# Memory attention and a Sinkhorn mixture of experts: the norm's epsilon in a preset column, one reduction for two, and four small products on GpSimd

## The chip, the cores and the metric

The kernel runs on one core of one Trainium2 chip. A core has five engines that work from queues of their own: TensorE (PE in the profile; its weight loads are PEld), VectorE (DVE), ScalarE (ACT), GpSimd (POOL) and SyncE (SP), which here issues the DMAs. Each engine takes its instructions in order; semaphores hold an instruction back until what it needs is done. The metric is device time in microseconds (us) of one execution, less is better.

## The reference

The first half is an attention with a memory, for B = 4 batches, H = 8 heads, S = 576 rows and D = 64 columns. The second half takes its output as the 2304 x 512 input of a mixture of 8 experts, whose router is normalised by Sinkhorn steps. The change lies in the first half, in the norm `mem_norm` and in the two lines that use it.

```python
scores = scale * np.matmul(q, k.transpose(0, 1, 3, 2))      # causal mask, then
a = np.exp(scores - scores.max(-1, keepdims=True))
a /= a.sum(-1, keepdims=True) + 1e-09
local = np.matmul(a, v)
q_p = np.where(q > 0, q, np.exp(q) - 1.0) + 1.0             # phi(q)
mem_ret = np.einsum('bhsd,bhde->bhse', q_p, M_prev)
mem_norm = np.einsum('bhsd,bhd->bhs', q_p, z_prev)[..., None] + 1e-06
g = 1.0 / (1.0 + np.exp(-beta))[None, :, None, None]
out = g * mem_ret / mem_norm + (1 - g) * local
```

## The kernel before

**Tiling.** Attention works on 16 pairs of heads (p = 0 to 15). A pair's 576 rows are four tiles of 128 rows with both heads side by side (128 columns), and a fifth tile in which the 64 left rows of the first head lie on partitions 0 to 63 and those of the second on 64 to 127, each in its own half of the columns, with zeros in the other half. So a per-row number of a pair is a 128 x 9 tile: eight columns for four tiles times two heads, and one for the fifth tile.

**One pair.** `qkt` transposes q and k and splits them into a high and a low part (L231). `phi_` makes phi(q): exp on ACT into `tmp` (L256), min with 1 on DVE (L257), max and add on DVE into `phi` (L258), and then POOL multiplies phi by z into `tmp` again (L261 for four tiles, L265 for the fifth). `nrm` sums `tmp` over the 64 columns (L274, and L277 for the fifth tile), adds 1e-6 (L278), takes the reciprocal (L279) and multiplies by the gate (L280); the result is `rm`. `pv_in` multiplies v by one minus the gate on POOL (L286, `vs`). `scores` multiplies q and k (L303), adds the mask and takes the smallest negated score on DVE (L317, two instructions for each tile of rows), and exponentiates on ACT (L324); `scores_tail` does the same for the fifth tile (L335, L341, L347). ACT writes the sums into `sum`, and the last of them is L347's.

`r_stats` adds 1e-9 to `sum` (L415), multiplies by `rm` (L416, `rms`), takes the reciprocal of the sum (L417, `rv`), and POOL then scales phi by `rms`: the fifth tile into `qn4` (L420, two instructions), the four others in place (L425). `r_trans` transposes `rv` (L433), `qn4` (L434) and the scaled phi (L455) on TensorE; the copies out of PSUM are L436, L452 and L456. The row of `rv` goes through DRAM by DMA and comes back as `rsb` (L447), broadcast over the partitions. `t_a` and `t_b` transpose the exponentials (L361, L379), copied out by L362, L367 and others. `pv` multiplies them with `vs` and the scaled phi with the memory matrix (L470, L475), and `comb`, all on POOL, multiplies by `rsb` (L494), rounds (L497) and subtracts (L498) to get the two parts of the second half's input.

**Order.** Each step carries a phase number, and the list of all steps is sorted by pair plus phase: load -1.6, qkt -0.40, phi_ -0.38, pv_in -0.36, nrm -0.10, scores 0, t_a 0.50, r_stats 0.70, t_b 0.80, r_trans 0.90, pv 0.95 and 1.15, comb 1.45. `w_task`, at 0.5, 1.0, 1.5 and 2.0, splits the first expert's weights on POOL (L115, L116), and from pair 5 on matmuls of the second half (L621, L636) and the router's logits fill in between. This list is the order on TensorE. On the other engines the scheduler chooses an order when the program is built, and it is then fixed.

**Buffers.** `phi`, `rm`, `vs`, `rr` have two buffers each, by the parity of the pair; `tmp` has one.

Of the kernel before, what the change touches and what calls it, by code (L numbers as in the profile page):

```python
# [8 lines left out]
F32 = mybir.dt.float32  # L9
F32R = mybir.dt.float32r  # L10
AF = mybir.ActivationFunctionType
ALU = mybir.AluOpType
AX = mybir.AxisListType
# [4 lines left out]
def kernel(  # L18
# [13 lines left out]
    nc = tc.nc  # L32
# [55 lines left out]
    gcol = ca.tile([128, HP, 9], F32, name="gcol")  # L88
# [82 lines left out]
    def attention():  # L171
        with ExitStack() as actx:
            ap1 = actx.enter_context(tc.tile_pool(name="ap1", bufs=1))
# [4 lines left out]
            qraw, kraw, vraw = (  # L178
                [ap1.tile([128, 5, 128], F32, name=f"{x}raw{j}") for j in range(2)] for x in "qkv"
            )  # L180
# [6 lines left out]
            e4t = ap1.tile([128, 2, 64], F32, name="e4t")  # L187
            e4 = ap1.tile([128, 576], F32, name="e4")
            qn4 = ap1.tile([128, 128], F32, name="qn4")

            for t_ in (*qraw, *kraw, *vraw):
                nc.vector.memset(t_[:, 4, :], 0.0)
            for t_ in (*mraw, *zb2, qn4, e4t):
                nc.vector.memset(t_, 0.0)

            st = [dict() for _ in range(NPAIR)]
            half = [slice(0, 64), slice(64, 128)]
# [51 lines left out]
                split_ps(kk[0][:, 576:704], kk[1][:, 576:704], tv[:, 1])  # L249

            def phi_(p):
                tmp = ap1.tile([128, 5, 128], F32, tag="tmp", name="tmp", bufs=1)
                phi = ap1.tile([128, 5, 128], F32, tag="phi", name="phi", bufs=2)
                st[p]["phi"], st[p]["tmp"] = phi, tmp
                zb = zb2[p % 2]
                nc.scalar.activation(out=tmp, in_=qraw[p % 2], func=AF.Exp)  # L256
                nc.vector.tensor_scalar_min(tmp, tmp, 1.0)  # L257
                nc.vector.scalar_tensor_tensor(  # L258
                    out=phi, in0=qraw[p % 2], scalar=0.0, in1=tmp, op0=ALU.max, op1=ALU.add
                )  # L260
                nc.gpsimd.tensor_tensor(  # L261
                    out=tmp[:, 0:4], in0=phi[:, 0:4],
                    in1=zb[:, 0:1].to_broadcast([128, 4, 128]), op=ALU.mult,
                )
                nc.gpsimd.tensor_tensor(  # L265
                    out=tmp[:, 4], in0=phi[:, 4], in1=zb[:, 1], op=ALU.mult
                )

            def nrm(p):
                hp = p % HP  # L270
                tmp = st[p].pop("tmp")
                rm = ap1.tile([128, 9], F32, tag="rm", name="rm", bufs=2)
                st[p]["rm"] = rm
                nc.vector.reduce_sum(  # L274
                    rm[:, 0:8], tmp[:, 0:4].rearrange("p t (h d) -> p (t h) d", h=2), axis=AX.X
                )
                nc.vector.reduce_sum(rm[:, 8:9], tmp[:, 4], axis=AX.X)  # L277
                nc.vector.tensor_scalar_add(rm, rm, 1e-6)  # L278
                nc.vector.reciprocal(out=rm, in_=rm)  # L279
                nc.vector.tensor_tensor(out=rm, in0=rm, in1=gcol[:, hp], op=ALU.mult)  # L280

            def pv_in(p):
                hp = p % HP
# [127 lines left out]
            def r_stats(p):  # L411
                phi = st[p]["phi"]
                rr = ap1.tile([128, 3, 9], F32, tag="rr", name="rr", bufs=2)
                den, rms, rv = (rr[:, j] for j in range(3))
                nc.vector.tensor_scalar_add(den, st[p]["sum"], 1e-9)  # L415
                nc.vector.tensor_tensor(out=rms, in0=st[p]["rm"], in1=den, op=ALU.mult)  # L416
                nc.vector.reciprocal(out=rv, in_=den)  # L417
                st[p]["rr"] = rr
                for h in range(2):
                    nc.gpsimd.tensor_tensor(  # L420
                        out=qn4[half[h], half[h]], in0=phi[half[h], 4, half[h]],
                        in1=rms[half[h], 8:9].to_broadcast([64, 64]), op=ALU.mult,
                    )
                ph = phi[:, 0:4].rearrange("p t (h d) -> p (t h) d", h=2)
                nc.gpsimd.tensor_tensor(  # L425
                    out=ph, in0=ph, in1=rms[:, 0:8].unsqueeze(2).to_broadcast([128, 8, 64]),
                    op=ALU.mult,
                )
# [60 lines left out]
            def comb(p, grp):  # L489
# [11 lines left out]

            atoms = [
                (-1.6, load), (-0.40, qkt), (-0.38, phi_), (-0.36, pv_in), (-0.10, nrm),
                (0.00, lambda p: scores(p, (3,))), (0.01, lambda p: scores(p, (2,))),
                (0.30, lambda p: scores(p, (1, 0))), (0.31, scores_tail),
                (0.50, t_a), (0.80, t_b), (0.70, r_stats), (0.90, r_trans),
                (0.95, lambda p: pv(p, 0)), (1.15, lambda p: pv(p, 1)),
                (1.45, lambda p: comb(p, 0)), (1.46, lambda p: comb(p, 1)),
# [437 lines left out]

    setup()
    attention()
    front.close()
    experts()  # L950
# [30 lines left out]
```

## Time and profile before

| what | value |
|---|---|
| device time, median of 3 runs | 1772.59 us (1772.06 to 1774.39) |
| span of the profiled execution, first to last instruction | 1770.6 us |
| device time of the runs less the span | 2.0 us |
| mean granted TensorE clock, as a share of full speed | 0.996 |
| TensorE busy | 1723.7 us, 97% of the span |
| DVE busy | 1289.0 us, 73% |
| POOL busy | 1166.0 us, 66% |
| ACT busy | 685.7 us, 39% |
| attention, by the trace | 0 to about 272 us |

The trace has the profiled execution's own time as its span; the runs lie 2.0 us above it, which is what lies around the first and the last instruction. A busy share here is an average over a first half in which five engines hand work to each other and a second half that is nearly all matmuls, so it says nothing of a single stage.

### The profile page before, as it was taken

Reading aid. Unit: us, or ns where it says so; the run is one execution under the profiler, and the core shown is the slowest. Engines: PE = TensorE matmul, PEld = TensorE weight load, DVE = VectorE, ACT = ScalarE, POOL = GpSimd, SP = SyncE. Lnnn points to the kernel's source line nnn. Section 1 sums busy time; section 2 is a strip of 40 time slices with the busy share of each in tenths; the row PEclk is TensorE's granted clock in tenths of the full one; section 3 lists DMA queues with packets and bytes.
Section 4 is the critical chain, followed back from the end, with each engine's and each line's share of the span. In section 5 each row is a group of like instructions: output and inputs, shape, how many; then the busy total and the mean of one; then the engine's idle time right before and its main releaser. Section 6 shows DMA issues by size and latency. Waiting matters only on the chain.

```text
span 1770.6 us, 26969 instructions
## 1 busy us (share of the span) xinstructions
PE 1723.7 (97%) x9381; PEld 1522.5 (86%) x9381; DVE 1289.0 (73%) x2371; ACT 685.7 (39%) x1550; POOL 1166.0 (66%) x1113
## 2 busy tenths in 40 slices
PE   5899999999999999999999999999999999999999
PEld 4677777889999999888899999998898999999998
DVE  6887873787777777767777777777667777777776
ACT  4766762233333333333333333333333333333332
POOL 4655543567777777676677777776676777777773
PEclk8999999999999999999999999999999999999999
DMA  4443414222222222214222222222142222222221
GB/s 109 105 103 96 114 41 149 57 70 71 72 66 61 65 72 72 72 49 142 72 71 61 65 66 72 72 72 72 48 143 72 65 61 66 72 72 72 72 60 48
DMA packets 154888, 135.55 MB, mean 77 GB/s; under 512 B 71424, under 2 KB 121728, under 8 KB 154752
## 3 DMA queue, kind: packets, MB, share of 16 engines
q1 hardware_dynamic: 154320, 133.05, 25.0%
q8 instruction: 74, 1.21, 0.3%
q10 hardware_dynamic: 432, 0.79, 0.1%
q14 instruction: 62, 0.51, 0.1%
HBM read 124.28 MB, written 9.51 MB: 76 GB/s over the span
## 4 chain that ended last, share of the span: by engine, by line
PE 81%; POOL 5%; DVE 4%; issue 4%; DMA 2%; ACT 2%; SPq 1%; POOLq 0%; ACTq 0%; DVEq 0%
PE s L636 40%; PE s L805 27%; PE f L805 9%; PE x L470 1%; ACT e L324 1%; DMA rsb<-rd 1%; PE s L303 1%; DVE hhl L790 1%; POOL tl L710 1%; POOL phi L425 1%; POOL w1l L756 1%; DVE acc L877 0%; PE s L621 0%; PE f L636 0%; POOL w2l L779 0%
## 5 line engine op out<-in xcount | busy, mean ns | idle before, releaser
L756 POOL TENSOR_TENSOR w1l<-raw,w1h 128x512 fp32r<-128x512 f32 x263 | 368.2, 1414 | 395.1 <-ACT w1h L755 394.9
L878 DVE SCALAR_TENSOR_TENSOR acc<-s,P,acc 128x512 f32<-128x512 f32 x504 | 369.2, 745 | 133.5 <-PE s L636 131.1
L636 PE MATMUL s<-w2h,hhh 128*128 128x512 f32 x1116 | 435.5, 390 | 6.0 <-DVE acc L878 5.9
L636 PE MATMUL s<-w2h,hhl 128*128 128x512 f32 x1116 | 436.1, 391 | 0.0
L636 PE MATMUL s<-w2l,hhh 128*128 128x512 f32 x1116 | 435.8, 391 | 0.0
L836 DVE TENSOR_TENSOR temps<-s,temps 128x384 f32<-128x384 f32 x447 | 242.5, 555 | 169.8 <-ACT w1h L755 83.0
L790 DVE SCALAR_TENSOR_TENSOR hhl<-temps,hhh 128x384 fp32r<-128x384 f32 x340 | 306.5, 901 | 0.0
L779 POOL TENSOR_TENSOR w2l<-raw,w2h 128x512 fp32r<-128x512 f32 x186 | 292.7, 1595 | 11.9 <-ACT w2h L778 11.9
L789 ACT ACTIVATE hhh<-temps 128x384 fp32r<-128x384 f32 x340 | 178.7, 526 | 297.8 <-DVE temps L836 289.9
L636 PEld LDWEIGHTS s<-w2h,hhh 128*128 128x128 f32 x1116 | 209.6, 188 | 50.6 <-DVE acc L878 9.5
L636 PEld LDWEIGHTS s<-w2h,hhl 128*128 128x128 f32 x1116 | 209.4, 188 | 44.0
L636 PEld LDWEIGHTS s<-w2l,hhh 128*128 128x128 f32 x1116 | 209.4, 188 | 41.5
L839 ACT COPY temps<-s 128x384 f32<-128x384 f32 x64 | 30.7, 480 | 413.7 <-PE s L805 412.6
L805 PE MATMUL s<-th,w1l 128*128 128x384 f32 x510 | 170.8, 335 | 1.5 <-POOL w1l L756 1.5
L805 PE MATMUL s<-tl,w1h 128*128 128x384 f32 x510 | 170.7, 335 | 0.8 <-POOL tl L710 0.8
L805 PE MATMUL s<-th,w1h 128*128 128x384 f32 x510 | 170.6, 334 | 0.0
L805 PE MATMUL s<-xh,w1l 128*128 128x384 f32 x480 | 161.7, 337 | 0.5 <-POOL w1l L751 0.5
L805 PE MATMUL s<-xh,w1h 128*128 128x384 f32 x480 | 161.7, 337 | 0.0
L805 PE MATMUL s<-xl,w1h 128*128 128x384 f32 x480 | 161.2, 336 | 0.0
L755 ACT CAST w1h<-raw 128x512 fp32r<-128x512 f32 x263 | 153.7, 615 | 3.7 <-issue 3.0
L836 DVE TENSOR_TENSOR temps<-f,temps 128x384 f32<-128x384 f32 x148 | 80.3, 555 | 55.3 <-PE f L805 26.2
L778 ACT CAST w2h<-raw 128x512 fp32r<-128x512 f32 x186 | 112.1, 607 | 0.0
(220 smaller groups left out, 2895.0 us busy)
## 6 DMA issues: line engine op xcount, KB each, us to landing
raw<-in_moe_w_dram SPq DMA_DIRECT2D x372, 256.0 KB
rsb<-rd SPq DMA_DIRECT2D x32, 144.0 KB
ydr<-wst SPq DMA_DIRECT2D x18, 256.0 KB
acc<-ydr SPq DMA_DIRECT2D x18, 256.0 KB
qraw<-in_q_dram SPq DMA_DIRECT2D x32, 128.0 KB
kraw<-in_k_dram SPq DMA_DIRECT2D x32, 128.0 KB
vraw<-in_v_dram SPq DMA_DIRECT2D x32, 128.0 KB
out_dram<-acc SPq DMA_DIRECT2D x15, 256.0 KB
```

What stands on the lines that cost most here:

```text
L303: nc.tensor.matmul(out=sp[h][:, at:at + w], lhsT=qq[x][half[h], 128 * i:128 * i + 128], rhs=kk[y][half[h], 0:w], start=(a == 0), stop=(a = ...
L636: nc.tensor.matmul(out=pt, lhsT=h_[:, f, cols], rhs=w[:, f], start=(n == 0), stop=(n == 5))
L755: nc.scalar.copy(out=wh[:, i:i + 2], in_=src)
L756: tt(out=wl[:, i:i + 2], in0=src, in1=f32(wh[:, i:i + 2]), op=ALU.subtract)
L778: nc.scalar.copy(out=wh[:, j], in_=raws[j])
L779: nc.gpsimd.tensor_tensor(out=wl[:, j], in0=raws[j], in1=f32(wh[:, j]), op=ALU.subtract)
L789: nc.scalar.activation(out=hh[:, f, c], in_=src, func=AF.Relu)
L790: late.append(lambda: nc.vector.scalar_tensor_tensor(out=hl[:, f, c], in0=src, scalar=0.0, in1=f32(hh[:, f, c]), op0=ALU.max, op1=ALU.subt ...
L805: nc.tensor.matmul(out=pt[:, 0:HT], lhsT=w[:, wi, k], rhs=x[:, k], start=(n == 0), stop=(n == total - 1),)
L836: nc.vector.tensor_tensor(out=o, in0=x, in1=y, op=ALU.add)
L839: nc.scalar.copy(out=X, in_=prod(q, [(0, b11)]))
L878: nc.vector.scalar_tensor_tensor(out=acc[:, j], in0=pt, scalar=P[:, t_, e:e + 1], in1=acc[:, j], op0=ALU.mult, op1=ALU.add,)
```

## The change

`tmp` becomes one tile for the whole attention, 65 columns for each tile and head in place of 64. The 65th column is preset once: 1e-6, and zero for the second half of the fifth tile. `phi_` writes exp straight into `phi` and works there in place, so that `tmp` only holds phi times z; POOL's product for four tiles becomes two instructions (one for each head), since the rows are now 65 apart. `nrm` takes one reduction over all ten groups of 65, which brings the epsilon with it, and adds the two columns of the fifth tile on POOL (128 x 1). Its product with the gate, and in `r_stats` the sum plus 1e-9 and the product with `rm`, go from DVE to POOL. Both reciprocals stay on DVE.

```diff
+            tmp = ap1.tile([128, 5, 2, 65], F32, name="tmp")
...
+            nc.vector.memset(tmp[:, :, :, 64:65], 1e-6)
+            nc.vector.memset(tmp[:, 4, 1, 64:65], 0.0)
...
-                tmp = ap1.tile([128, 5, 128], F32, tag="tmp", name="tmp", bufs=1)
...
-                nc.scalar.activation(out=tmp, in_=qraw[p % 2], func=AF.Exp)
-                nc.vector.tensor_scalar_min(tmp, tmp, 1.0)
+                nc.scalar.activation(out=phi, in_=qraw[p % 2], func=AF.Exp)
+                nc.vector.tensor_scalar_min(phi, phi, 1.0)
                 nc.vector.scalar_tensor_tensor(
-                    out=phi, in0=qraw[p % 2], scalar=0.0, in1=tmp, op0=ALU.max, op1=ALU.add
-                )
+                    out=phi, in0=qraw[p % 2], scalar=0.0, in1=phi, op0=ALU.max, op1=ALU.add
+                )
+                pv_ = phi.rearrange("p t (h d) -> p t h d", h=2)
+                zv = zb.rearrange("p t (h d) -> p t h d", h=2)
+                for h in range(2):
+                    nc.gpsimd.tensor_tensor(
+                        out=tmp[:, 0:4, h, 0:64], in0=pv_[:, 0:4, h],
+                        in1=zv[:, 0:1, h].to_broadcast([128, 4, 64]), op=ALU.mult,
+                    )
                 nc.gpsimd.tensor_tensor(
-                    out=tmp[:, 0:4], in0=phi[:, 0:4],
-                    in1=zb[:, 0:1].to_broadcast([128, 4, 128]), op=ALU.mult,
-                )
-                nc.gpsimd.tensor_tensor(
-                    out=tmp[:, 4], in0=phi[:, 4], in1=zb[:, 1], op=ALU.mult
+                    out=tmp[:, 4, :, 0:64], in0=pv_[:, 4], in1=zv[:, 1], op=ALU.mult
                 )
...
-                rm = ap1.tile([128, 9], F32, tag="rm", name="rm", bufs=2)
+                rm = ap1.tile([128, 10], F32, tag="rm", name="rm", bufs=2)
...
-                nc.vector.reduce_sum(
-                    rm[:, 0:8], tmp[:, 0:4].rearrange("p t (h d) -> p (t h) d", h=2), axis=AX.X
-                )
-                nc.vector.reduce_sum(rm[:, 8:9], tmp[:, 4], axis=AX.X)
-                nc.vector.tensor_scalar_add(rm, rm, 1e-6)
-                nc.vector.reciprocal(out=rm, in_=rm)
-                nc.vector.tensor_tensor(out=rm, in0=rm, in1=gcol[:, hp], op=ALU.mult)
+                nc.vector.reduce_sum(rm, tmp.rearrange("p t h d -> p (t h) d"), axis=AX.X)
+                nc.gpsimd.tensor_tensor(
+                    out=rm[:, 8:9], in0=rm[:, 8:9], in1=rm[:, 9:10], op=ALU.add
+                )
+                nc.vector.reciprocal(out=rm[:, 0:9], in_=rm[:, 0:9])
+                nc.gpsimd.tensor_tensor(
+                    out=rm[:, 0:9], in0=rm[:, 0:9], in1=gcol[:, hp], op=ALU.mult
+                )
...
-                nc.vector.tensor_scalar_add(den, st[p]["sum"], 1e-9)
-                nc.vector.tensor_tensor(out=rms, in0=st[p]["rm"], in1=den, op=ALU.mult)
+                nc.gpsimd.tensor_scalar_add(den, st[p]["sum"], 1e-9)
+                nc.gpsimd.tensor_tensor(out=rms, in0=st[p]["rm"][:, 0:9], in1=den, op=ALU.mult)
                 nc.vector.reciprocal(out=rv, in_=den)
```

The changed program is five lines longer ahead of the attention's steps, so that L256 to L258 of before are L258 to L260 there, L279 is L282, L286 is L291, L317 is L322, L415 to L425 are L420 to L430 and L494 is L499; phi times z is L266 and L270, the one reduction L278, the sum of the two columns L279, the gate on POOL L283. TensorE's order stays as it was. What the scheduler makes of the rest is shown at three places.

POOL's queue at the first two pairs; vs_123 and vs_124 are the products of pairs 0 and 1 (L286), zb_126 belongs to pair 1. Before:

```order
L261 TENSOR_TENSOR tmp<-phi,zb_126 128x512
L265 TENSOR_TENSOR tmp<-phi,zb_126 128x128
L286 TENSOR_TENSOR vs<-vraw_123,ogb 128x640
L286 TENSOR_TENSOR vs<-vraw_124,ogb 128x640
L420 TENSOR_TENSOR qn_136<-phi,rr 64x64 x2
L425 TENSOR_TENSOR phi<-phi,rr 128x512
```

And now:

```order
L279 TENSOR_TENSOR rm<-rm 128x1
L420 TENSOR_SCALAR rr<-sum 128x9
L283 TENSOR_TENSOR rm<-rm,gcol 128x9
L421 TENSOR_TENSOR rr<-rm,rr 128x9
L425 TENSOR_TENSOR qn_136<-phi,rr 64x64 x2
L430 TENSOR_TENSOR phi<-phi,rr 128x512
L291 TENSOR_TENSOR vs<-vraw_123,ogb 128x640
L291 TENSOR_TENSOR vs<-vraw_124,ogb 128x640
L266 TENSOR_TENSOR tmp<-phi,zb_126 128x4x64 x2
L270 TENSOR_TENSOR tmp<-phi,zb_126 128x2x64
```

The scaling of pair 0's phi stands ahead of both products with v, and pair 1's phi times z behind them.

POOL's queue around the scaling of pair 1's phi, from the product with v for pair 2 on; L115 and L116 are the weights, L494 to L498 are `comb` of pair 0. Before:

```order
L286 TENSOR_TENSOR vs<-vraw_123,ogb 128x640
L115 CAST w1h_72<-wst 128x512
L116 TENSOR_TENSOR w1l_73<-wst,w1h_72 128x512
L494 TENSOR_TENSOR xc<-xc,rsb 128x256
L494 TENSOR_TENSOR xc<-xc,rsb 128x320
L497 CAST xh<-xc 128x256
L497 CAST xh<-xc 128x320
L498 TENSOR_TENSOR xl<-xc,xh 128x256
L498 TENSOR_TENSOR xl<-xc,xh 128x320
L420 TENSOR_TENSOR qn_136<-phi,rr 64x64 x2
L425 TENSOR_TENSOR phi<-phi,rr 128x512
```

And now:

```order
L291 TENSOR_TENSOR vs<-vraw_123,ogb 128x640
L115 CAST w1h_72<-wst 128x512
L279 TENSOR_TENSOR rm<-rm 128x1
L116 TENSOR_TENSOR w1l_73<-wst,w1h_72 128x512
L283 TENSOR_TENSOR rm<-rm,gcol 128x9
L115 CAST w1h_72<-wst 128x512
L116 TENSOR_TENSOR w1l_73<-wst,w1h_72 128x512
L420 TENSOR_SCALAR rr<-sum 128x9
L421 TENSOR_TENSOR rr<-rm,rr 128x9
L425 TENSOR_TENSOR qn_136<-phi,rr 64x64 x2
L499 TENSOR_TENSOR xc<-xc,rsb 128x256
L499 TENSOR_TENSOR xc<-xc,rsb 128x320
```

Behind these stand the four other instructions of `comb` of pair 0 (L502, L503), and only then L430, the scaling of pair 1's phi: `comb` went from ahead of pair 1's `qn4` to between it and the rest of phi. L279 of pair 2's norm stands behind a product with v and a cast of weights.

DVE's queue behind the last reduction of scores of pair 5 (L341 and its accumulator); L627 and L632 are the second half's hidden layer, L367 and L362 copies that free PSUM. Before:

```order
L341 ISA mn 128x1
L415 TENSOR_SCALAR rr<-sum 128x9
L416 TENSOR_TENSOR rr<-rm,rr 128x9
L417 RECIPROCAL rr<-rr 128x9
L627 SCALAR_TENSOR_TENSOR hl_77<-f,hh_76 128x512
L367 COPY e_133<-s 128x128
L362 COPY eB<-s 128x3x128 x2
```

And now:

```order
L346 ISA mn 128x1
L422 RECIPROCAL rr<-rr 128x9
L632 SCALAR_TENSOR_TENSOR hl_77<-f,hh_76 128x512
L372 COPY e_133<-s 128x128
L367 COPY eB<-s 128x3x128 x2
```

The reciprocal stands where it stood, but what it reads (`rr`, from L420) now comes from POOL, where L420 stands behind `comb` of the pair ahead.

## Rows read from the trace of the kernel before

**Rows 1.** Busy time of each engine by stretch (us, count), granted clock, DMA.

```profile
20.00:100.00 80.00, 65.15 (x547) 47.50 (x546) 69.16 (x220) 51.85 (x160) 51.73 (x66) 0.94 0.44 107
100.00:272.00 172.00, 167.19 (x1347) 130.05 (x1347) 134.53 (x458) 115.77 (x344) 90.02 (x126) 1.00 0.33 87
272.00:1770.00 1498.00, 1481.83 (x7445) 1337.03 (x7441) 1074.01 (x1650) 510.25 (x1028) 1020.29 (x908) 1.00 0.23 73
```

The columns behind the stretch's length are PE, PEld, DVE, ACT and POOL, then the granted TensorE clock, the DMA share and GB/s.

**Rows 2.** What TensorE waited for, 20 to 100 us: total, times, longest.

```profile
PE s L434 <- POOL qn L420: 6.0, 2, 5.7
PE s L455 <- POOL phi L425: 3.0, 4, 0.8
```

**Rows 3.** Tiles rm and rr on DVE: shortest/median/longest ns of one.

```profile
L416 DVE TENSOR_TENSOR rr<-rm,rr x16: 153/328/1442, 26.6 to 265.0; 128x9 f32<-128x9 f32 x16
...
L278 DVE TENSOR_SCALAR rm<-rm x15: 176/798/1471, 31.1 to 244.5; 128x9 f32<-128x9 f32 x15
```

**Rows 4.** Prices: groups up to 480 us (busy us, mean ns), and one memset.

```profile
L256 ACT ACTIVATE tmp<-qraw 128x640 f32<-128x640 f32 x16 | 11.8, 736 | 14.2 <-DMA kraw<-in_k_dram 7.9 <-DVE rm L277 4.0 <-DMA qraw<-in_q_dram 2.3
L420 POOL TENSOR_TENSOR qn<-phi,rr 64x64 f32<-64x64 f32 x32 | 9.3, 291 | 6.4 <-DVE rr L416 3.4 <-DVE rr L417 1.4
L257 DVE TENSOR_SCALAR tmp<-tmp 128x640 f32<-128x640 f32 x16 | 8.1, 504 | 3.8 <-ACT tmp L256 3.8
...
0.24 0.10 POOL L965 MEMSET const-float32-0.0<- 128x1 f32 x1 [0.24 <-issue]
```

**Rows 5.** Timeline, pair 0: start, us, instruction, [idle before it <- releaser].

```profile
11.94 0.69 DVE L274 TENSOR_REDUCE rm<-tmp 128x8 f32<-128x512 f32 x1 [5.27 <-POOL tmp L261]
...
15.13 0.69 DVE L317 CUSTOM_DVE_ANT_0 e<-s,mask 128x512 f32<-128x512 f32 x1 [0.43 <-PE s L303]
...
26.52 3.02 POOL L286 TENSOR_TENSOR vs<-vraw,ogb 128x640 f32<-128x640 f32 x2 [2.77 <-DVE rm L280]
...
31.34 1.12 PE L455 MATMUL s<-ident,phi 128*128 128x128 f32 x4 [0.65 <-POOL phi L425]
```

**Rows 6.** Timeline, pair 1.

```profile
36.34 0.69 DVE L317 CUSTOM_DVE_ANT_0 e<-s,mask 128x512 f32<-128x512 f32 x1 [0.91 <-PE s L303]
...
40.63 0.41 DVE L317 CUSTOM_DVE_ANT_0 e<-s,mask 128x256 f32<-128x256 f32 x1
...
42.57 1.55 POOL L494 TENSOR_TENSOR xc<-xc,rsb 128x256 f32<-128x256 f32 x2
...
43.95 0.19 ACT L347 ACTIVATION_READ_ACCUMULATOR e<-e,mn 128x1 f32 x1
...
44.82 1.55 POOL L498 TENSOR_TENSOR xl<-xc,xh 128x256 fp32r<-128x256 f32 x2
...
48.31 0.66 PE L455 MATMUL s<-ident,phi 128*128 128x128 f32 x4 [0.79 <-POOL phi L425]
```

**Rows 7.** Timeline, from pair 1's transposes to pair 2's.

```profile
49.00 0.59 ACT L456 COPY qp<-s 128x512 f32<-128x512 f32 x1 [0.91 <-PE s L455]
...
50.60 1.30 POOL L261 TENSOR_TENSOR tmp<-phi,zb 128x512 f32<-128x512 f32 x1 [2.35 <-DVE phi L258]
...
62.14 1.05 POOL L425 TENSOR_TENSOR phi<-phi,rr 128x512 f32<-128x512 f32 x1
```

**Rows 8.** Timeline, pairs 9 and 6.

```profile
167.65 1.55 POOL L498 TENSOR_TENSOR xl<-xc,xh 128x256 fp32r<-128x256 f32 x2
168.34 0.20 DVE L417 RECIPROCAL rr<-rr 128x9 f32<-128x9 f32 x1
...
169.34 0.33 PE L245 MATMUL s<-ident,kraw 128*128 128x128 f32 x1 [0.67 <-DVE e L367]
...
122.24 0.33 PE L245 MATMUL s<-ident,kraw 128*128 128x128 f32 x1 [0.80 <-ACT eB L362]
```

**Rows 9.** Busy time by stretch, columns as in rows 1, in the second half.

```profile
784.00:787.00 3.00, 0.96 (x4) 0.70 (x5) 2.77 (x4) 0.83 (x1) 3.00 (x3) 1.00 0.04 16
787.00:790.00 3.00, 3.00 (x11) 3.00 (x10) 1.16 (x3) 1.30 (x3) 3.00 (x3) 0.51 0.37 118
```

More of the change, by code (lines that the diff above doesn't have):

```diff
@@ L251, in phi_ @@
             def phi_(p):
-                tmp = ap1.tile([128, 5, 128], F32, tag="tmp", name="tmp", bufs=1)
                 phi = ap1.tile([128, 5, 128], F32, tag="phi", name="phi", bufs=2)
-                st[p]["phi"], st[p]["tmp"] = phi, tmp
+                st[p]["phi"] = phi
                 zb = zb2[p % 2]
-                nc.scalar.activation(out=tmp, in_=qraw[p % 2], func=AF.Exp)
-                nc.vector.tensor_scalar_min(tmp, tmp, 1.0)
+                nc.scalar.activation(out=phi, in_=qraw[p % 2], func=AF.Exp)
+                nc.vector.tensor_scalar_min(phi, phi, 1.0)
                 nc.vector.scalar_tensor_tensor(
-                    out=phi, in0=qraw[p % 2], scalar=0.0, in1=tmp, op0=ALU.max, op1=ALU.add
+                    out=phi, in0=qraw[p % 2], scalar=0.0, in1=phi, op0=ALU.max, op1=ALU.add
                 )
-                nc.gpsimd.tensor_tensor(
-                    out=tmp[:, 0:4], in0=phi[:, 0:4],
-                    in1=zb[:, 0:1].to_broadcast([128, 4, 128]), op=ALU.mult,
-                )
-                nc.gpsimd.tensor_tensor(
-                    out=tmp[:, 4], in0=phi[:, 4], in1=zb[:, 1], op=ALU.mult
+                pv_ = phi.rearrange("p t (h d) -> p t h d", h=2)
[5 more added lines that the diff above has]
+                    )
+                nc.gpsimd.tensor_tensor(
+                    out=tmp[:, 4, :, 0:64], in0=pv_[:, 4], in1=zv[:, 1], op=ALU.mult
                 )
@@ L270, in nrm @@
                 hp = p % HP
-                tmp = st[p].pop("tmp")
-                rm = ap1.tile([128, 9], F32, tag="rm", name="rm", bufs=2)
+                rm = ap1.tile([128, 10], F32, tag="rm", name="rm", bufs=2)
                 st[p]["rm"] = rm
-                nc.vector.reduce_sum(
-                    rm[:, 0:8], tmp[:, 0:4].rearrange("p t (h d) -> p (t h) d", h=2), axis=AX.X
-                )
-                nc.vector.reduce_sum(rm[:, 8:9], tmp[:, 4], axis=AX.X)
-                nc.vector.tensor_scalar_add(rm, rm, 1e-6)
-                nc.vector.reciprocal(out=rm, in_=rm)
-                nc.vector.tensor_tensor(out=rm, in0=rm, in1=gcol[:, hp], op=ALU.mult)
+                nc.vector.reduce_sum(rm, tmp.rearrange("p t h d -> p (t h) d"), axis=AX.X)
+                nc.gpsimd.tensor_tensor(
+                    out=rm[:, 8:9], in0=rm[:, 8:9], in1=rm[:, 9:10], op=ALU.add
+                )
+                nc.vector.reciprocal(out=rm[:, 0:9], in_=rm[:, 0:9])
+                nc.gpsimd.tensor_tensor(
+                    out=rm[:, 0:9], in0=rm[:, 0:9], in1=gcol[:, hp], op=ALU.mult
+                )
             def pv_in(p):
```

## The prediction

> **What bounds the kernel now.** I read the busy time by stretch first, to find where a change to attention can still move the end. From 272 us on TensorE is busy 1481.8 of 1498 us [rows 1]; nothing is edited there, so the time moves by what attention's end moves. From 100 to 272 us TensorE is busy 167.2 of 172 us, so 4.8 us at most can be won there. From 20 to 100 us it is idle 14.9 us: there other engines set the pace. Next I read TensorE's waits in that stretch: 9.0 of the 14.9 us are waits for POOL's two scalings of phi, L420 and L425, one of them of 5.7 us [rows 2]. So the chain that decides runs through POOL: phi times z, the products with v, the weights and `comb`, all in one queue with the scalings. The reader is to see that DVE's small products are not what TensorE waits for by name; they are a step of the way to L420.
>
> **What is taken away.** Two of DVE's small instructions are odd: L416 takes 153 ns at best but 328 at the median and 1442 at most, L278 176, 798 and 1471 [rows 3]. Their shapes never change: L416 of pair 0, one of the long ones, began at 26.6, just behind the start of POOL's L286 at 26.52 [rows 3, 5]. I read them as held until the running POOL instruction ends, and the change takes L278, L280, L415 and L416 off DVE, 64 instructions over the 16 pairs. L277 goes into the longer reduction. What a stall cost TensorE is at most the stretch by which the next step was late, and that is counted below, place by place.
>
> **What is added on POOL.** Four small products for each pair. No row shows a POOL product of nine columns. Below it is bounded by the memset of 128x1, 0.10 us, above by L420's 64x64 at 0.29 [rows 4]. I take 0.15 and 0.07 for the hand-over, 0.22 in all, since nine columns are nearer to one than to 64. Phi times z becomes two instructions of 256 columns for one of 512 at 1.30 [rows 7]; two of 256 and 320 take 1.55 (L494 [rows 6]), so I take 1.5: +0.2.
>
> **Pair 0.** POOL's scaling waited at 26.52 for DVE's L280, then did both products with v (3.02 us), and only then L420 and L425; L455 began at 31.34 [rows 5]. Now the scaling is ahead of both: -3.0. L274 stood on DVE ahead of the splits of q and k and held them 5.27 us [rows 5]; it now stands behind them. Pair 0's first scores, at 15.13, come about 1.1 earlier, and the gates that POOL waits for with them. L455 of pair 0 at 27.2: -4.1.
>
> **Pair 1.** The two products with v (3.0) now run after L430, to 30.2, and pair 1's phi times z (2.0) after them, to 32.2. The one reduction (0.7, as L274) waits for that and stands on DVE ahead of the score reductions, which so begin at 33.7, not 36.34 [rows 6]. Four of them end at 35.9, pair 2's phi at 36.7, its product with z at 38.7. Then POOL does vs of pair 2 (1.5, half of L286's two) and a cast of weights (0.6, from the 0.7 that `comb`'s two casts of 576 columns fill between L494 and L498 [rows 6]) ahead of L279, whose result DVE's reciprocal waits for; behind the reciprocal stand the last score reductions: 41.3, where they began at 40.63 [rows 6]. So the lead is gone: +0.7. The last sum, at 44.14 (43.95 and 0.19), comes at about 44.9. L420, L421 and L425 take 0.22, 0.22 and 0.66: 46.0. Now `comb` of pair 0 is behind them and takes 3.8 to 3.9 (before it ran from 42.57 to 46.37, while the sums were made and divided: that was its cover [rows 6]). 49.9, and L430 takes 1.05 to 51.0: L455 of pair 1 at 51.1 for 48.31 [rows 6]: **+2.8**. Bounds: 0 if the DMA-fed parts come earlier and comb starts at once, 3.9 if all of comb is late.
>
> **Pair 2.** From 48.3 to 63.2 (62.14 and 1.05) POOL is busy but for 2.35 us ahead of phi times z [rows 7]. That gap is a chain: L455, then L258, which writes the `phi` that L455 has read. L256 and L257 had been done into `tmp` meanwhile. Now they write `phi` too, so they come behind L455 and L456: 0.59, then 0.74 and 0.50 [rows 4, 7], less what L257 overlapped: +1.1. The product with z adds 0.2, the four small ones 0.9, the hand-over to vs 0.4: **+2.6**, and **+0.5** for pair 3 by the same chain with a little slack; none for pair 4, whose queue has no weights.
>
> **Pairs 5 to 15.** L422 stands where L417 stood, but waits for L420, which stands behind `comb`. At pair 9 L498 ends at 169.20 (167.65 and 1.55), while L417 began at 168.34 and L245 waited at 169.34 for L367 behind it [rows 8]. With L420's 0.22 and a hand-over L422 begins at 169.5: 1.15 later, and what stands behind it (L632, L372, L367) too, for which L245 waits. Pairs 5, 8 and 12 have the same order and L417 ahead of comb's end by like amounts: 4 x 1.15 = 4.6 (bounds 0, if the copies have slack, and 6). Two pairs with 0.1 of slack in the scaling lose 0.3 each. Given back: pairs 6 and 10, where L245 waited 0.80 at 122.24 [rows 8] for copies that DVE's stalled products held, 0.8 each, and 0.6 at the last pair. **+3.0** net.
>
> **The clock.** After 3 us in which TensorE was busy only 0.96, the next 3 us were granted 0.51 of full speed, 1.2 GHz, with TensorE busy throughout: 1.5 us lost [rows 9]. Now there is a gap of nearly 4 us ahead of pair 1's L455, which had 0.79. I take one more such stretch, a little longer: **+1.7** (0 to 4).
>
> **Sum.** 2.8 + 2.6 + 0.5 + 3.0 + 1.7 = 10.6 on the profiled span of 1770.6: 1781.2, and 2.0 around it: **1783.2** against the median of 1772.59. The second half begins later by as much and is otherwise the same.
>
> **A rule weighed.** The nearest rows gave 0.15 us for a small product on POOL, about what DVE needs unstalled (0.153 to 0.176 [rows 3]). The Trainium skill, "GPSIMD Engine Reference", section Key points, has VectorE about twice as fast at elementwise work. By that a product would be an estimated 0.35, and where some 15 of them lie on the path the sum would be 3 us more, 1786. No row here has the same product on both engines.
>
> **The rivals.**
>
> *Faster, about 1764.* The stalls of DVE go (a long L416 or L278 costs up to 1.3 over its shortest [rows 3]), and pair 0's lead of 4.1 stays, because DVE's queue, free of them, keeps POOL fed. Then -4.1, three stalls of 1.1 among pairs 1 to 3, -1.6 at pairs 6 and 10: -9.0. It decides if POOL has over 1 us of slack a pair in 30 to 63 us. For it: the stalls are real, and 9 us of waits there have POOL's name [rows 2]. Against it: in pair 2's loop POOL's only slack is a wait on `phi` [rows 7], which the change makes longer. The Trainium skill, "SBUF — State Buffer", section Who interferes with whom, bears on this rival: a DVE product with two SBUF inputs, or a copy-like one in a two-port mode, and a GpSimd instruction lock each other out, a reduction does not. The trace agrees as far as L416 and L278 stretch to eight and nine times their shortest [rows 3].
>
> *No change, about 1773.* The pace from 60 us on is TensorE's own, and what POOL loses in pairs 1 and 2 is filled from its list, or pair 0's lead of 4.1 pays for pair 2. For it: 97% busy from 100 us on [rows 1]. Against it: TensorE's order is fixed, and L455 is in it ahead of pair 2's products.
>
> *Much slower, about 1789.* TensorE's gaps ahead of L455 lower the clock in three or four pairs, at 1.5 to 2 each [rows 9], and comb's 3.9 is late in pair 2 as well.
>
> **How the numbers follow.** The forecast's own terms, with their bounds, go from 1776 to 1789. I give it 0.56, much slower 0.08, no change 0.2, faster 0.16. To leave out no more than 2 in 10 the range must reach through no change and a little into the faster case: 1768 to 1788. What a measurement can tell is about 0.2%, 3.5 us: faster than 1769.0 has 0.15, within it 0.2, slower than 1776.1 has 0.65.
>
> **What would show it.** After: TensorE idle before pair 0's L460 at about 27 rather than 31; the scaling of pair 1 (L425, L430) split by `comb`, with L460 of pair 1 near 51 after a wait of some 4 us for POOL; L258 of pair 3 behind L460 of pair 1, and POOL's wait before L266 near 3.4; L422 in pairs 5, 8, 9 and 12 waiting for POOL's L420 and TensorE's transposes of k (L248) waiting for L372; TensorE at half clock once more between 50 and 60. Small POOL products of 0.10 to 0.29. I am wrong if L460 of pair 2 comes no later than 63.2, if TensorE is idle under 15 us from 20 to 100, or if the second half begins before 272.

## The result, and the profile after

| | before | changed |
|---|---|---|
| device time, median of 4 runs | 1773.49 us (1772.06 to 1775.50) | 1784.67 us (1783.32 to 1787.42) |
| span of the profiled execution | 1770.6 us | 1782.2 us |

The ratio is 1.0062, with a 95% interval of 1.0048 to 1.0077: slower by 11 us, where 1783.2 had been forecast. From the page of the changed kernel, the span and the row with busy time, share of the span and instructions of each engine:

```profile
span 1782.2 us, 26967 instructions
...
PE 1730.5 (97%) x9381; PEld 1529.0 (86%) x9381; DVE 1259.3 (71%) x2293; ACT 686.2 (39%) x1550; POOL 1180.0 (66%) x1193
```

DVE has 29.7 us less to do and POOL 14.0 more. The shares hardly move, so the page alone would not tell which way the time went. The busy time by stretch does (columns as in rows 1; below the first three rows, the stretches around four gaps):

```profile
20.00:100.00 80.00, 60.72 (x466) 44.26 (x464) 48.85 (x172) 45.05 (x138) 53.57 (x88) 0.89 0.41 97
100.00:272.00 172.00, 164.80 (x1335) 128.42 (x1335) 120.17 (x403) 116.12 (x339) 96.62 (x171) 0.99 0.34 88
272.00:1770.00 1498.00, 1484.26 (x7492) 1339.18 (x7491) 1073.32 (x1666) 515.61 (x1046) 1025.26 (x919) 1.00 0.24 73
23.00:26.00 3.00, 0.00 (x0) 0.00 (x0) 2.86 (x14) 0.46 (x2) 1.80 (x4) 1.00 0.48 111
27.00:33.00 6.00, 5.48 (x26) 3.65 (x28) 1.11 (x2) 1.59 (x3) 5.06 (x7) 0.50 0.25 57
46.00:50.00 4.00, 0.21 (x2) 0.00 (x0) 1.90 (x8) 0.80 (x3) 4.00 (x7) 1.00 0.43 101
51.00:54.00 3.00, 3.00 (x17) 1.77 (x18) 1.32 (x2) 1.59 (x3) 0.27 (x1) 0.50 0.44 107
65.00:67.00 2.00, 0.03 (x1) 0.00 (x0) 0.86 (x3) 1.16 (x5) 1.92 (x4) 1.00 0.06 13
68.00:74.00 6.00, 5.14 (x23) 3.19 (x25) 2.07 (x6) 1.59 (x3) 2.03 (x4) 0.50 0.28 66
178.00:179.50 1.50, 0.00 (x0) 0.00 (x0) 0.80 (x3) 0.00 (x0) 1.20 (x5) 1.00 0.62 142
180.25:183.75 3.50, 3.50 (x10) 2.67 (x9) 2.05 (x5) 1.59 (x5) 0.54 (x1) 0.55 0.31 71
```

From 20 to 100 us TensorE is idle 19.3 us (80 less 60.72) against 14.9 in [rows 1], from 100 to 272 us 7.2 against 4.8, and four times a gap is followed by a stretch at half the clock (0.50, 1.2 GHz; the last is 0.55 on average over the window shown). The kernel before had one such stretch in attention, at 26 to 36 us, which answers to the first of the four. What TensorE waited for from 20 to 100 us (total, times, longest; the rows that answer to [rows 2]):

```profile
PE s L460 <- POOL phi L430: 5.6, 3, 4.1
PE s L439 <- POOL qn L425: 4.0, 2, 3.6
PE s L366 <- ACT e L329: 2.8, 2, 2.5
PE s L438 <- DVE rr L422: 2.5, 1, 2.5
```

The places are those of the prediction, in the timeline of the changed kernel at pairs 0, 1 and 2:

```profile
23.95 0.37 POOL L283 TENSOR_TENSOR rm<-rm,gcol 128x9 f32<-128x9 f32 x1 [4.14 <-DVE gcol L152]
...
27.14 0.47 PE L460 MATMUL s<-ident,phi 128*128 128x128 f32 x1 [0.79 <-POOL phi L430]
...
45.51 0.73 POOL L499 TENSOR_TENSOR xc<-xc,rsb 128x256 f32<-128x256 f32 x1
...
49.26 1.04 POOL L430 TENSOR_TENSOR phi<-phi,rr 128x512 f32<-128x512 f32 x1
...
50.36 0.33 PE L460 MATMUL s<-ident,phi 128*128 128x128 f32 x1 [4.14 <-POOL phi L430]
...
53.73 0.74 POOL L266 TENSOR_TENSOR tmp<-phi,zb 128x256 f32<-128x256 f32 x1 [3.43 <-DVE phi L260]
...
57.52 1.55 POOL L291 TENSOR_TENSOR vs<-vraw,ogb 128x640 f32<-128x640 f32 x1 [1.94 <-PE x L475]
...
67.55 0.27 PE L438 MATMUL s<-ident,rr 128*9 128x128 f32 x1 [2.52 <-DVE rr L422]
```

Pair 0 is 4.2 us early (27.14 for 31.34), pair 1 late by 2.05 (50.36 for 48.31 [rows 5, 6]). The transposes of the scaled phi (L455, now L460) mark the way of each pair; their starts in the changed kernel less those of before, each from the one profiled execution (the times of 27 executions of the kernel before lie between 1769.4 and 1776.8 us, so differences of one or two microseconds in the text below are not certain by themselves):

| pair | 0 | 1 | 2 | 3 | 4 | 8 | 9 | 12 | 15 |
|---|---|---|---|---|---|---|---|---|---|
| us | -4.20 | 2.05 | 6.10 | 8.36 | 7.93 | 9.09 | 11.92 | 12.78 | 12.11 |

So 8.4 us are lost up to pair 3, 2.8 at pair 9 alone, and nothing behind attention: 11.6 at the end of the span.

### The profile page after: what moved, and what is told of

It is laid out like the page before. It is cut to its first block, busy times and chain, and to the rows that moved or that the text cites. A ratio compares the mean times of both kernels' runs of the same rounds, so it can differ in the third digit from the quotient of the medians.

```text
span 1782.2 us, 26967 instructions
## 1 busy us (share of the span) xinstructions
PE 1730.5 (97%) x9381; PEld 1529.0 (86%) x9381; DVE 1259.3 (71%) x2293; ACT 686.2 (39%) x1550; POOL 1180.0 (66%) x1193
## 3 DMA queue, kind: packets, MB, share of 16 engines
q8 instruction: 74, 1.21, 0.3%
## 4 chain that ended last, share of the span: by engine, by line
PE 82%; POOL 7%; issue 4%; DVE 3%; DMA 2%; ACT 1%; SPq 0%; POOLq 0%; ACTq 0%; DVEq 0%
PE s L641 40%; PE s L810 27%; PE f L810 9%; PE x L475 1%; PE s L308 1%; POOL xc L499 1%; DMA rsb<-rd 1%; POOL xl L503 1%; POOL tl L715 1%; PE s L366 1%; POOL tmp L266 1%; POOL vs L291 1%; POOL w1l L761 1%; PE f L641 1%; DVE hhl L795 1%
## 5 line engine op out<-in xcount | busy, mean ns | idle before, releaser
L784 POOL TENSOR_TENSOR w2l<-raw,w2h 128x512 fp32r<-128x512 f32 x186 | 292.2, 1589 | 12.0 <-ACT w2h L783 11.6
```

Of the source, the lines that this page charges most:

```text
L784: nc.gpsimd.tensor_tensor(out=wl[:, j], in0=raws[j], in1=f32(wh[:, j]), op=ALU.subtract)
```

## The experiments

All were timed beside the kernel before. The first theory is the prediction's four terms: `comb` ahead of pair 1's L430, phi in place, the products in POOL's queue with L422 behind `comb`, and the clock. Its rivals: only POOL's added work counts, or phi in place is the whole loss.

**1. Exp and min through `tmp` again, the rest as changed.**

```diff
-                nc.scalar.activation(out=phi, in_=qraw[p % 2], func=AF.Exp)
-                nc.vector.tensor_scalar_min(phi, phi, 1.0)
+                ex = tmp[:, :, :, 0:64]
...
+                nc.scalar.activation(out=ex, in_=qv, func=AF.Exp)
+                nc.vector.tensor_scalar_min(ex, ex, 1.0)
...
```

> The changed kernel, but exp and min go through the 64 columns of tmp again (as before the change), not through phi. My theory (four terms: comb ahead of pair 1's scaling, phi in place, POOL's queue, the clock): the gap ahead of phi times z of pair 3 falls from 3.43 to about 2.4 us and the one of pair 4 from 3.90 to about 2.9; 1 to 3 us less than the changed kernel, 1782 to 1784. The rival that only POOL's added work counts: no difference, 1784.7. The rival that phi in place is the whole loss: about 1774.

Measured: 1790.79 us, ratio 1.0103 (1.0088 to 1.0118), 6 us more than the changed kernel: all three were wrong. The timeline of POOL shows why my term gave nothing back at pair 2:

```profile
53.80 0.73 POOL L268 TENSOR_TENSOR tmp<-phi,zb 128x256 f32<-128x256 f32 x1 [1.71 <-DVE phi L263]
...
59.33 1.55 POOL L293 TENSOR_TENSOR vs<-vraw,ogb 128x640 f32<-128x640 f32 x1 [3.68 <-PE x L477]
```

The gap ahead of phi times z falls from 3.43 to 1.71, as it should, and the next instruction in the queue, the product with v, then waits 3.68 for its buffer, not 1.94. From pair 1's transposes to pair 2's it is 18.99 us here and 18.98 in the changed kernel. The gap was real, and behind another wait of the same size.

**2. `comb` behind the scaling.**

```diff
-                (1.45, lambda p: comb(p, 0)), (1.46, lambda p: comb(p, 1)),
+                (1.75, lambda p: comb(p, 0)), (1.76, lambda p: comb(p, 1)),
```

> The changed kernel, with comb's phase 1.75 and 1.76 for 1.45 and 1.46: in POOL's queue only pairs 1 and 2 change, L430 of pair 1 stands right behind its L425 and comb of pair 0 behind both, and in pair 2 the scaling stands ahead of L503. My theory: L460 of pair 1 at about 46.5, not 50.36, TensorE's 4.1 us wait and the half clock behind it go, and the 3.4 us that POOL waits for phi take comb in; 5 to 9 us less than the changed kernel, 1776 to 1780. Rival, POOL's work alone: the same work, so 1784.7. Rival, phi in place alone: the same, 1784.7.

Measured: 1777.65 us, ratio 1.0039 (1.0025 to 1.0053), by the medians 7 us less than the changed kernel with the same instructions, and within the range of my theory. The timeline of pair 1:

```profile
45.59 1.04 POOL L430 TENSOR_TENSOR phi<-phi,rr 128x512 f32<-128x512 f32 x1
46.59 1.56 POOL L499 TENSOR_TENSOR xc<-xc,rsb 128x256 f32<-128x256 f32 x2
...
46.69 0.66 PE L460 MATMUL s<-ident,phi 128*128 128x128 f32 x4
```

L460 has lost its wait of 4.14 and comes at 46.69. The place of `comb` in POOL's queue is shown to be a cause; that only POOL's work counts is out.

**3. The four products back on DVE; column, one reduction and phi in place stay** (`nc.gpsimd` is `nc.vector` again in L279, L283, L420 and L421).

> The changed kernel with all four small products back on DVE; the preset column, the one reduction and phi in place stay. The scheduler's order goes back to that of before at pairs 0 to 2. My theory: pair 0 gives its 4 us back, pair 1's comb is ahead again, no L422 waits for comb; what is left is phi in place and the second instruction of phi times z, 2 to 4 us over before: 1775 to 1778. Rival, POOL's added products are all of it: 1773.5. Rival, phi in place is all of it: 1784.

Measured: 1770.87 us, ratio 0.9990 (0.9980 to 0.9999). Below my range: phi in place and the second instruction of phi times z do not cost what I gave them.

**4. The column alone** (3 and 1 together).

> Only the preset column, the one reduction and the split phi times z of the change: products on DVE and exp and min through tmp. My theory: within 1 us of before, 1773 to 1775, since POOL has 0.2 us more a pair and DVE two instructions less. Both rivals: 1773.5. If it is faster than before by more than 2 us, DVE's time counts more than I gave it.

Measured: 1772.61 us, ratio 1.0002 (0.9993 to 1.0010). One reduction for two, the epsilon in it and the split product cost and win nothing beyond that interval. Runs 3 and 4 differ in phi in place alone, and with it the time is 1.7 us less; their two intervals overlap, so this difference alone shows no gain. It does show that phi in place does not cost what I gave it at pairs 2 and 3. The traces say where it wins: from pair 4 to pair 15 run 3 gains 3.9 us on before, run 4 only 0.7.

**5. DVE makes its own sum for the reciprocal.**

```diff
-                nc.vector.reciprocal(out=rv, in_=den)
+                nc.vector.tensor_scalar_add(rv, st[p]["sum"], 1e-9)
+                nc.vector.reciprocal(out=rv, in_=rv)
```

> The changed kernel, but the reciprocal L422 no longer reads POOL's L420: DVE adds 1e-9 to the sum a second time itself, right ahead of it. POOL's queue and work are those of the changed kernel. My theory (L422 waits behind comb in POOL's queue and holds the copies behind it): the steps at pairs 5, 8, 9 and 12 (0.6, 0.9, 2.8, 0.9 us against before) and the half clock at 180 us go, pairs 1 to 3 stay: 3 to 5 us less than the changed kernel, 1780 to 1782. Rival, POOL's added work alone: 1784.7. Rival, DVE gains from having no product there to be stalled: slower than the changed kernel, 1785 to 1790.

Measured: 1777.40 us, ratio 1.0018 (1.0009 to 1.0027), 7.3 us less than the changed kernel, and more than I expected. POOL still does all four products. In the changed kernel pair 9 looks like this:

```profile
176.78 1.55 POOL L503 TENSOR_TENSOR xl<-xc,xh 128x256 fp32r<-128x256 f32 x2
...
178.42 0.25 POOL L420 TENSOR_SCALAR rr<-sum 128x9 f32<-128x9 f32 x1
178.70 0.21 DVE L422 RECIPROCAL rr<-rr 128x9 f32<-128x9 f32 x1 [4.85 <-POOL rr L420]
...
178.83 0.63 DVE L632 SCALAR_TENSOR_TENSOR hl<-f,hh 128x512 fp32r<-128x512 f32 x1
...
179.38 0.28 DVE L372 COPY e<-s 128x128 f32<-128x128 f32 x1
...
179.72 0.33 PE L248 MATMUL s<-ident,kraw 128*128 128x128 f32 x1 [1.96 <-DVE e L372]
```

and here, where L422 is DVE's own sum and L423 the reciprocal:

```profile
174.05 0.67 DVE L422 TENSOR_SCALAR rr<-sum 128x9 f32<-128x9 f32 x1 [0.99 <-ACT e L352]
...
174.75 0.21 DVE L423 RECIPROCAL rr<-rr 128x9 f32<-128x9 f32 x1
...
176.22 1.56 POOL L504 TENSOR_TENSOR xl<-xc,xh 128x256 fp32r<-128x256 f32 x2
...
176.79 0.27 PE L248 MATMUL s<-ident,kraw 128*128 128x128 f32 x1
...
177.87 0.25 POOL L420 TENSOR_SCALAR rr<-sum 128x9 f32<-128x9 f32 x1
```

The reciprocal is done 3 us ahead of L420, and L248 waits for nothing. The half clock at 180 us is gone with the gap. From pair 4 to pair 15 the changed kernel lost 4.2 us on before; this one wins 4.0, so L422's wait is worth 8.2 us there. Between runs 2 and 6, which differ in the same edit, it is 7.2.

**6. Both, 2 and 5.**

> Both: comb behind the scaling in pairs 1 and 2, and DVE's own sum for the reciprocal; all four products of the change stay on POOL. My theory: the two gains add up (7.0 and 3 to 5 us of 11.9): 1773 to 1775, the time of before, with POOL doing the same work as in the changed kernel. Rival, POOL's added work alone: 1784.7, or 1777.7 if only the place of comb matters.

Measured: 1769.67 us, ratio 0.9973 (0.9962 to 0.9985): 15.0 us less than the changed kernel, below my range, and faster than before with POOL's added work still there. By the medians that is about the sum of 7.0 and 7.3; by the ratios the two single edits win 4.1 and 7.8 us and both together 15.8, each good to some 3.5 us, and at pair 15's transposes it is 6.0, 7.2 and 14.8. So the gains add up, as far as these numbers can tell.

**7. The products alone, in the kernel before** (L280, L415 and L416 on POOL).

> The kernel before with three of its small products on POOL (the gate, 1e-9 on the sum, the product of both); no preset column, two reductions, exp and min through tmp. In POOL's queue pair 0's scaling is ahead of the products with v, as in the changed kernel, but comb stays ahead of pair 1's scaling. The run with exp through tmp was 6 us slower than the changed kernel, so I have given up that phi in place costs time; it wins some. My theory now: pair 1 about 2 us earlier than in the changed kernel, the waits of L417 for comb as there, exp through tmp 4 to 6: 1783 to 1788. Rival, the products are all of the loss and phi in place is nothing: 1782 to 1785. If it is at 1774 or below, the loss was in the other edits.

Measured: 1786.42 us, ratio 1.0072 (1.0058 to 1.0085). That is within my range and above the rival's. The products without the other edits lose at least as much as the whole change.

**8. Run 3 with `pv_in` at 0.40.** That is behind the load of the pair after next, so its products take that pair's v; its time is read, and it is no version to keep.

> The third run (products on DVE, preset column, phi in place) with pv_in's phase 0.40 for -0.36, so that pair 0's scaling stands ahead of the products with v on POOL, as the changed kernel had it, with comb still ahead of pair 1's scaling. If the lead of pair 0 is worth something where POOL's queue has slack: 2 to 4 us less than the third run, 1767 to 1769, faster than both kernels. If the lead is lost as in the changed kernel: 1770 to 1772.

Measured: 1770.21 us, ratio 0.9976 (0.9967 to 0.9985), above the first range and inside the second, that the lead is lost. Pair 0's lead of 4.1 us is still 2.4 at pair 1 and 0.8 at pair 2, and at pair 5 it is a loss of 3.5, behind stretches of half clock from 58 and from 92 us. The lead can be kept for two pairs; it doesn't reach the end.

**9. Phi in place alone, in the kernel before.**

> The kernel before with only exp and min written into phi in place of tmp; POOL's queue keeps its order. My first theory had this edit cost 1.1 us in each of pairs 2 and 3; the first, third and fourth run have overturned that (1.7 us between two kernels that differ in it alone, the other way). Now: tmp no longer has to wait for the reduction of the pair ahead, so from pair 5 on exp comes earlier, 3 to 5 us less there, 1 to 2 lost at pairs 2 and 3: 1769 to 1772. If it costs on the whole: 1775 or more.

Measured: 1770.22 us, ratio 0.9985 (0.9976 to 0.9995). The first two rows are the reduction of pair 9's norm and the score reduction behind it in the kernel before:

```profile
158.88 0.69 DVE L274 TENSOR_REDUCE rm<-tmp 128x8 f32<-128x512 f32 x1 [1.41 <-POOL tmp L261]
159.49 0.68 DVE L317 CUSTOM_DVE_ANT_0 e<-s,mask 128x512 f32<-128x512 f32 x1
```

and here:

```profile
159.80 0.68 DVE L317 CUSTOM_DVE_ANT_0 e<-s,mask 128x512 f32<-128x512 f32 x1
...
161.97 0.68 DVE L274 TENSOR_REDUCE rm<-tmp 128x8 f32<-128x512 f32 x1
```

The scheduler has put the score reductions first, and DVE no longer stands for 1.41 us in front of POOL's product. The order comes with the edit; that exp comes later there (it waits for the buffer of phi) is what I take for the scheduler's reason, and no run shows it. DVE's waits for that product from 100 to 272 us (total, times, longest), first in the kernel before, then in run 1, where exp goes through `tmp` again:

```profile
DVE rm L274 <- POOL tmp L261: 12.6, 9, 1.4
...
DVE rm L280 <- POOL tmp L272: 17.7, 9, 2.0
```

Neither this kernel nor the changed one has such a wait in that stretch. From pair 5 to pair 15 this kernel wins 3.4 us.

**10. The first weights later, the rest as changed.**

```diff
-                seq.append((0.5 + 0.5 * j, lambda j=j: w_task(j)))
+                seq.append((2.4 + 0.6 * j, lambda j=j: w_task(j)))
```

> The changed kernel with the first expert's weights at phases 2.4, 3.0, 3.6 and 4.2 for 0.5 to 2.0: out of pairs 1 and 2, POOL's queue has 7.6 us less there, the products wait for no weights, and comb of pair 0 stands ahead of pair 1's L420 and all of it. If the loss of pairs 1 to 3 (8.4 us with the lead that is lost) is made by what shares POOL's queue there: 5 to 8 us less than the changed kernel, 1777 to 1780. Rival, the products' own time and L422's wait: 0 to 2 less, 1783 to 1785.

Measured: 1779.19 us, ratio 1.0031 (1.0021 to 1.0041), 5.5 less than the changed kernel, within the range of the first case. Pair 2's transposes are 1.1 us ahead of before, not 6.1 behind; at pairs 3 and 4, where the weights now are, 4.2 of it are lost.

**11. The sixth run with the weights late.**

> The sixth run (comb behind the scaling, DVE's own sum) with the weights late as well. If pairs 1 and 2 there still pay for the weights on POOL: 2 to 5 us less than the sixth run, 1765 to 1768. If not: 1769 to 1771.

Measured: 1772.92 us, ratio 0.9997 (0.9988 to 1.0006), above both ranges. The weights only move the loss: pair 3 is 2.2 us behind before here and 0.7 in the sixth run. Run 6 keeps the lowest ratio of the runs that compute the whole reference; the intervals of runs 3 and 9 overlap with its own.

## Why the prediction held, and where it did not

**Pair 0, -4.1:** measured -4.20. The two causes hold, and runs 4 and 7 show them one by one: the one reduction without the products has pair 0 at -1.21, the products alone at -3.14. But that the size came out is in part luck. POOL's wait for the gate ended at 23.95 where it had ended at 26.52, 2.6 us earlier and not 1.1, and the two small products then took 1.4 us up to the scaling at 25.33, which the term left out.

**Pair 1, +2.8:** measured +2.05; L430 stood behind `comb` as forecast, and run 2 shows it by its removal.

**The lead lost:** the last score reductions of pair 1 began at 40.58 for a forecast 41.3, behind a reciprocal that waited 1.38 us for POOL's L279.

**Pair 2, +2.6:** measured +4.05 with 1.5 of clock in it, and the step that failed is "That gap is a chain": the chain is there, but it does not set the pace. The gap ahead of phi times z was forecast at 2.35 + 1.1 and measured at 3.43. But the product with v behind it waits for TensorE in any case, the casts of weights that used to fill that wait stand behind it in the queue, and run 1 took 1.72 from the one wait and gave 1.74 to the other. Of the term the four small products and the queue remain.

**Pair 3, +0.5:** measured +2.26. The half clock at 68 to 74 us lies here (2.6 us by its row); in runs 2 and 6, which have no half clock between pair 2's transposes and pair 3's, pair 3 loses 0.4.

**Phi in place** was counted only as a cost. It is a gain, 3 us in run 9 on the kernel before and 6 between run 1 and the changed kernel; the 1.7 between runs 4 and 3 points the same way and is within the noise. I had the scheduler's order of DVE in hand and read in it only the place of L422, not that the reduction had moved behind the score reductions.

**Pairs 5 to 15, +3.0:** measured +4.2 from pair 4 on. The mechanism held: the pairs named, 5, 8, 9 and 12, lose 0.6, 0.9, 2.8 and 0.9 there, though at 8 and 12 it is the matmuls of the router's logits (L554) that wait for L372, not L248. The size was off: L422's wait is worth 8.2 us where I had 4.6, of which 1.6 is the half clock at 180 us (3.5 us at 0.55). What I had "given back" at 2.2 was 4.0, mostly by phi in place (runs 3 and 4). The group of L422 in the changed kernel up to 272 us (busy us, mean ns, idle before it), and the reciprocal of the norm:

```profile
L282 DVE RECIPROCAL rm<-rm 128x9 f32<-128x9 f32 x16 | 3.4, 216 | 7.3 <-POOL rm L279 7.1
...
L422 DVE RECIPROCAL rr<-rr 128x9 f32<-128x9 f32 x15 | 3.2, 213 | 29.6 <-POOL rr L420 29.6
```

In the kernel before the products that left DVE were busy 31.8 us, stalls included:

```profile
L278 DVE TENSOR_SCALAR rm<-rm 128x9 f32<-128x9 f32 x16 | 13.1, 816 | 0.4
...
L416 DVE TENSOR_TENSOR rr<-rm,rr 128x9 f32<-128x9 f32 x16 | 7.2, 450 | 0.3
L415 DVE TENSOR_SCALAR rr<-sum 128x9 f32<-128x9 f32 x16 | 7.2, 449 | 7.1 <-ACT e L347 7.1
...
L280 DVE TENSOR_TENSOR rm<-rm,gcol 128x9 f32<-128x9 f32 x16 | 4.3, 269 | 0.5
```

At the shortest of each (0.153 to 0.175 us) the 64 would be an estimated 10.6 us, so some 21 us were stall. The stalls are gone, as the faster rival said, and 36.7 us of waits for POOL stand where they were: if the stalls are what the prediction took them for, DVE exchanged being held up by the POOL instruction that runs for waiting on a queue of POOL instructions.

**The clock, +1.7:** forecast as one stretch, there are three more than before. By the rows, busy time less what the granted clock allows is 3.00 x 0.50 + 5.14 x 0.50 + 3.50 x 0.45 = 5.6 us. If all of that was lost time, the sum of 10.6 came near 11.6 with two errors against each other: 4 us too little for the clock, and about 3 too much for the waits (8.9 forecast, 6.0 left). That the total is so near is then luck. How much of the 5.6 was lost stays open: run 3 has two stretches of half clock more than before, at 50 to 54 and 67 to 71 us, and is not slower.

**The small products' price,** 0.15 and 0.07: measured higher. POOL's four, up to 285 us in the changed kernel:

```profile
L420 POOL TENSOR_SCALAR rr<-sum 128x9 f32<-128x9 f32 x16 | 4.0, 250 | 7.8 <-ACT e L352 6.6
L421 POOL TENSOR_TENSOR rr<-rm,rr 128x9 f32<-128x9 f32 x16 | 3.9, 246 | 1.3
L283 POOL TENSOR_TENSOR rm<-rm,gcol 128x9 f32<-128x9 f32 x16 | 3.4, 215 | 4.5 <-DVE gcol L152 4.1 <-DVE rm L282 0.3
L279 POOL TENSOR_TENSOR rm<-rm 128x1 f32<-128x1 f32 x16 | 3.3, 205 | 16.2 <-DVE rm L278 14.0 <-DMA rsb<-rd 1.1 <-DMA kraw<-in_k_dram 1.1
```

By their medians, 0.249 (L420) and 0.206 us (L421, whose mean holds one of 0.85), they are 1.4 and 1.3 times the shortest of the same kind on DVE, 0.176 and 0.153 [rows 3]. The Trainium skill, "GPSIMD Engine Reference", section Key points, has about twice; these runs lie between that and the nearest row that I took. Run 6 shows that this price is not the loss: it pays all of it and is faster than before.

What stays open: why run 11 is no faster than before although pairs 1 and 2 gain, beyond the place where its loss lies; and how much of pair 2's loss each of the small products has, since no run moved them one by one.

## What to carry to other kernels

Moving small instructions to another engine moves their results into that engine's queue: ask what stands ahead of the producer there, and what stands behind the consumer that now waits. Here the work cost nothing that a change of two phase numbers and one repeated addition of nine columns did not win back. Where a term is a gap that will grow, look for the next wait behind it; if that one ends at the same time anyway, the term is nothing.

## What the runs showed that I had not expected

The half clock can follow a short gap: at 178 us TensorE was idle for 2 us, the clock of the 1.5 us shown was still 1.00, and from 180.25 it was 0.55 on average over 3.5 us of unbroken matmuls. A gap that costs 2 us so cost up to 3.6. But it does not follow each of them. In run 10 L248 has a gap of 2.3 us at the same pair, and the clock behind it stays at 1.00 (columns as in rows 1):

```profile
172.80:175.00 2.20, 0.00 (x0) 0.00 (x0) 0.98 (x4) 0.00 (x0) 1.88 (x6) 1.00 0.52 119
175.25:178.75 3.50, 3.50 (x20) 2.90 (x19) 2.37 (x6) 2.07 (x6) 0.86 (x1) 1.00 0.23 51
```

The changed kernel's own gap of 2.5 us ahead of L366, which ends at 41.65, is followed by none either. So what half clock a change brings could not be read here from the length of a gap.

A POOL product of one column (205 ns) costs nearly as much as one of nine (215 to 250 ns).
